# V of the second attention as one tile per head: 128x32 PV products, shared pools and a new table of rankings

## The chip, the cores and the metric

The kernel runs on one core of a Trainium2 chip. The core has five engines with instruction streams of their own: TensorE (PE; its weight loads are shown apart, as PEld), VectorE (DVE), ScalarE (ACT), GpSimd (POOL) and SyncE (SP), which here only issues transfers. Sixteen DMA engines move data between the device's memory (HBM) and the core's memory (SBUF, 128 partitions); PE writes its results to PSUM, eight banks of 128 partitions x 512 float32. The metric is the device time of one execution in microseconds (us); lower is better.

## What is computed (the reference)

Two attention blocks with caches, A and B, on 16 sequences of 32 tokens, model width 1024, 32 query heads of 128. A has 4 heads of keys and values, each used by 8 query heads; B has 32. The cache has 1024 keys per head. All inputs are bfloat16.

```python
def ref(x, k_cache, v_cache, wq, wo):        # A: 4 kv heads repeated 8 times, B: 32
    q = (x @ wq).reshape(B, Sq, H, Dh).transpose(0, 2, 1, 3)
    scores = einsum("bhqd,bhkd->bhqk", q, k) * (Dh ** -0.5)
    p = softmax(scores, axis=-1)
    o = einsum("bhqk,bhkd->bhqd", p, v)
    return o.transpose(0, 2, 1, 3).reshape(B, Sq, H * Dh) @ wo
out = concatenate([ref_A, ref_B], axis=-1)
```

B's keys and values are most of the bytes: 16 x 32 x 1024 x 128 x 2 bytes = 134 MB each. Nothing of them is used twice.

## The kernel before, in words

The work of both attentions is cut into quads: four (sequence, head) combinations of 32 tokens, whose scores fill 128 partitions x 1024 keys, two PSUM banks. Each attention has 128 quads. A quad's steps are: scores (PE; scoresA at L1003, scoresB at L1035), negative maximum (DVE, L1046), exponential with row sum (ACT, L1059), transposition of P (PE, L1071 for A and L1105 for B), evacuation of P^T to SBUF (ACT or DVE, L659), PV (PE, L1091 for A and L1124 for B), reciprocal (DVE, L1173), normalisation by the row sum (ACT L1182 or DVE L1183), transposition of O (PE, L1190 for A and L1198 for B), and evacuation into OTA_sb or OTB_sb (L659). When a group is complete, its output projection follows (oproj, L831), added up over blocks in `acc` (L843, L852, L847). Query projections (L743, L762), the transposition of A's keys on PE (L977) and a reshuffling of B's queries (L773, L786) are spread over the steps.

B's quads go in pairs (pairB). A pair holds two sequences x four heads. Its K comes as four tiles of 512 KB, each of two adjacent heads: 1024 keys of a head on 64 partitions, 16 keys per partition. Such a tile is transposed in place by DVE in blocks of 32x32 (L984). V comes in the same shape, four tiles of two heads each (st_dmaVB, tile_src). So PV works on tiles of 64 partitions: `st_pvB` runs, for each of 16 key chunks, four products with 64x64 weights from P^T and 256 columns of V (two heads of one tile side by side). Half of each result belongs to the wrong head; the transposition of O (two products with `rowsel`, a masked identity) picks the right half. Both quads of a pair share P2_sb and PT2_sb. The last pair has a version of its own, `st_last` (L1143, L1161, L1162, L1165): it takes V in halves so that part of the projection can start before the last tiles are there.

SBUF holds 8 slots of K and 6 of V for B. From pair 51 (LATE) on, space that is no longer needed (wq_sb, xT_sb, half of QT_sb) gives four more homes to K and four to V (home_k, home_v). All loads are issued by SP in one queue, in a fixed order: a load that has to wait for its slot keeps back all that follow it. `load` writes each transfer such that one descriptor reads 16 KB (V) or 8 KB (K) of contiguous HBM.

The order on every engine, and who takes a step that ACT or DVE could take, is decided when the program is built. `list_schedule` replays the program with a table of durations (DUR, PACKET, DMA_FIRST and so on), counts instruction fetches of PE in blocks (FETCH_BLOCK, FETCH_US), and takes at each step the ready operation with the highest rank; banks and slots of the pools (SLOTS) are handed out in that replay. There are 16 variants of the rank (RANKS); TUNE names the variant for each stretch of 77 operations (WINDOW).

```python
SLOTS = {"bank": 8, "P": 2, "P2": 1, "PT": 2, "PT2": 2, "stat": 8, "O": 2, "O2": 3}
turn = len(order) // WINDOW
turn = TUNE[turn] if turn < len(TUNE) else 0
```

Of the kernel before, what the change touches and what calls it, by code (L numbers as in the profile page):

```python
# [30 lines left out]
PE_MODE = {"scoresB": 2, "Qshuf": 2, "Qshuf2": 2, "PVB": 3, "PVBh": 3}  # L31
MODE_IN = 0.094
MODE_OUT = {0: 0.0, 2: 0.18, 3: 0.1}
PE_INSTR = {"scoresB": 32, "scoresA": 2, "PT_trA": 8, "PT_trB": 8, "PVA": 16, "PVB": 32, "PVBh": 32, "OT_tr": 2, "OT_trB": 4, "KTA_tr": 16, "Qshuf": 16, "Qshuf2": 16,
            "qprojA": 4, "qprojB": 4, "oprojA": 4, "oprojB": 4, "xT_tr": 16}
FETCH_BLOCK = 252
FETCH_US = 6.2
# [9 lines left out]
TUNE = (6, 7, 1, 5, 6, 8, 8, 8, 8, 8, 8, 11, 5, 15, 1, 9, 0, 1, 5, 1, 7, 14,  # L47
        15, 12, 12, 10, 12, 12, 15, 3, 12, 14, 7, 13, 13, 13, 13, 13, 7, 6, 10, 1, 12, 10,
        3, 12, 0, 11, 9, 12, 7, 13, 12, 11, 12, 3, 4, 10, 14, 9, 9, 10, 4, 0, 0)
# [11 lines left out]
    "scoresB": (0.232, 0.20), "scoresA": (0.216, 0.20), "PT_trA": (0.48, 0.22), "PT_trB": (0.48, 0.22), "PVA": (0.45, 0.22), "PVB": (0.437, 0.22), "PVBh": (0.22, 0.22),  # L61
    "OT_tr": (0.056, 0.22), "OT_trB": (0.112, 0.22), "KTA_tr": (0.45, 0.22), "Qshuf": (0.39, 0.20), "Qshuf2": (0.235, 0.20), "qprojA": (0.432, 0.20), "qprojB": (0.432, 0.20),
    "oprojA": (0.432, 0.20), "oprojB": (0.432, 0.20), "xT_tr": (0.45, 0.22),
    "exp": (1.10, 0.12), "PT_ev@act": (0.466, 0.13), "norm@act": (0.25, 0.13), "normB@act": (0.36, 0.13), "OT_ev@act": (0.11, 0.13), "OTB_ev@act": (0.17, 0.13), "KTA_ev@act": (0.466, 0.13),
    "qA_ev@act": (0.47, 0.13), "qB_ev@act": (0.478, 0.13), "QR_ev@act": (0.478, 0.13), "acc0@act": (0.47, 0.13), "acc0@dve": (0.58, 0.12), "xT_ev@act": (0.90, 0.13),
    "o_fin@act": (0.47, 0.13),
    "KBt_tr": (1.15, 0.11), "max": (1.12, 0.11), "recip": (0.06, 0.11), "norm@dve": (0.265, 0.13), "normB@dve": (0.40, 0.13), "PT_ev@dve": (0.58, 0.12),
    "OT_ev@dve": (0.13, 0.12), "OTB_ev@dve": (0.2, 0.12), "KTA_ev@dve": (0.58, 0.12), "QBt_tr": (0.345, 0.10), "acc+": (0.58, 0.12), "accF": (0.59, 0.12),
    "qA_ev@dve": (0.58, 0.12), "qB_ev@dve": (0.58, 0.12), "xT_ev@dve": (0.60, 0.12), "o_fin@dve": (0.58, 0.12), "QR_ev@dve": (0.58, 0.12),
# [3 lines left out]
PACKET = {"kb_dma": (4096, 0.1592), "vb_dma": (4096, 0.1592), "outh_dma": (1024, 0.049), "wqh_dma": (1024, 0.049)}  # L73
PACKET_DEFAULT = (2048, 0.0847)
DMA_ISSUE = 0.45
DMA_FIRST = 1.4
DMA_LAST = 0.8


def dma_time(op):  # L80
    size, us = PACKET.get(op.name, PACKET_DEFAULT)
    return op.dur / size * us / 16
# [32 lines left out]
SLOTS = {"bank": 8, "P": 2, "P2": 1, "PT": 2, "PT2": 2, "stat": 8, "O": 2, "O2": 3}  # L115
# [12 lines left out]
class Prog:  # L128
# [120 lines left out]
    def list_schedule(self, lat=0.05, look=LOOK):  # L249
# [137 lines left out]
        dma_free = [0.0]  # L387
# [7 lines left out]
        pe_pos = [0]  # L395
        pe_have = {0: 0.0, 1: 0.0}

        def fetch_wait(i, st, commit=False):
            if ops[i].eng != "pe" or not FETCH_US:
                return 0.0  # L400
            n_ = PE_INSTR[ops[i].name]
            p0 = pe_pos[0]
            ex = 0.0
            b = p0 // FETCH_BLOCK + 1
            while b * FETCH_BLOCK <= p0 + n_ - 1:
                tb = st + ex + ops[i].dur[0] * (b * FETCH_BLOCK - p0) / n_
                a = pe_have.get(b, 0.0)
                if a > tb:
                    ex += a - tb
                    tb = a  # L410
                if commit:
                    pe_have[b + 1] = tb + FETCH_US
                b += 1
            if commit:
                pe_pos[0] = p0 + n_
            return ex
# [136 lines left out]
def build(nc, pa, pb, out):  # L553
# [34 lines left out]
    with stack:  # L588
# [21 lines left out]
        VB_sb = sb("VB_sb", [P, NVB, 16 * Dh], BF)  # L610
# [4 lines left out]
        P2_sb = sb("P2_sb", [P, SLOTS["P2"], 2 * Sk], BF)  # L615
        PT2_sb = sb("PT2_sb", [P, SLOTS["PT2"], Sk], BF)
        O2_sb = sb("O2_sb", [P, SLOTS["O2"], 2, Dh], BF)
        rowsel = sb("rowsel", [P, 2, P], BF)
        PT_sb = sb("PT_sb", [P, SLOTS["PT"], NCH, P], BF)
# [25 lines left out]

        pr.add("pool", lambda g: g.memset(rowsel[:], 0.0), writes=["rowsel"], name="c0")
        for r_ in range(4):
            pr.add("pool", lambda g, r_=r_: g.tensor_copy(rowsel[32 * r_:32 * r_ + 32, r_ % 2, 32 * r_:32 * r_ + 32], ident[32 * r_:32 * r_ + 32, 32 * r_:32 * r_ + 32]),
                   reads=["ident"], writes=["rowsel"], name="c1")
# [102 lines left out]
        def qprojB(m_, G):  # L752
# [5 lines left out]
            for j0 in range(0, DJ, JS):  # L758
# [6 lines left out]
                pr.add("pe", e_qp, reads=ws + [("xT", 1, G)] + ([("xV", 0), ("xV", 1)] if m_ == NMSB - 1 else []), writes=[v], claims=[("Qtok", (m_ * NG + G) % NQT)], name="qprojB", dur=0.225 * JS,  # L765
# [148 lines left out]
        def st_dmaKB(x):  # L914
            if x < 2 * NIT:
                kind, sl = home_k(x)
                pr.step, was = 2 * ((x - NKB) // 4) if x >= NKB else pr.step, pr.step
                pr.add("sp", lambda e: load(e, tile_k(x), tile_src("k", x), 2), writes=[(kind, sl)], dma_key=f"{kind.lower()}{sl}", name="kb_dma",
# [8 lines left out]
        def home_v(x):  # L927
            if x >= V_LAST:
                return ("KB", kb_of(x - 8))
            if x < XV:  # L930
                return ("VB", x % NVB)
            r = (x - XV) % (NVB + 4)
            return ("xV" if r < 2 else "QV", r % 2) if r < 4 else ("VB", (XV + r - 4) % NVB)
# [10 lines left out]

        def tile_k(x):
# [3 lines left out]
        def tiles_v(x, w):  # L949
            kind, sl = home_v(x)  # L950
            if kind == "xV":
                return xT_sb[:, 1, :, :].rearrange("p (i j) t -> p i (j t)", i=2)[:, sl:sl + w, :]
            if kind == "QV":
                return QT_sb[:, 0, :, :, :].rearrange("p (i b) a q -> p i (b a q)", i=2)[:, sl:sl + w, :]
            return (KB_sb if kind == "KB" else VB_sb)[:, sl:sl + w, :]

        def tile_v(x):
            return tiles_v(x, 1)[:, 0, :]

        def st_dmaVB(x):  # L960
            kind, sl = home_v(x)
            pr.step, was = 2 * ((x - NVB) // 4) if x >= NVB else pr.step, pr.step
            pr.add("sp", lambda e: load(e, tile_v(x), tile_src("v", x), 4), writes=[(kind, sl)],
                   dma_key=f"{kind.lower()}{sl}", name="vb_dma", dur=2 * Sk * Dh * 2, wtag={(kind, sl): ("V", x)})
# [18 lines left out]
        def st_ktrB(x):  # L983
            pr.add("dve", lambda e: e.transpose(tile_k(x).bitcast(F32), tile_k(x).bitcast(F32)),  # L984
                   writes=[home_k(x)], name="KBt_tr", rtag={home_k(x): x}, wtag={home_k(x): ("T", x)})
# [8 lines left out]
        def st_scoresA(q):  # L994
# [3 lines left out]
            if True:  # L998
# [3 lines left out]
                for u in range(2):  # L1002
                    pr.add("pe", lambda e, u=u: e.matmul(bank(vS[u]), qt[:, q.b, q.hh0:q.hh0 + 4, :].rearrange("p a q -> p (a q)"),  # L1003
                                                         KTA_sb[:, sl, u * 512:(u + 1) * 512], start=True, stop=True),
                           reads=[("QT", q.s % 2, q.hh0 + a) for a in range(4)] + [("KTA", sl)] + ([("QV", 0), ("QV", 1)] if q.s == NSB - 2 else []), writes=vS, name="scoresA", dur=0.225,
                           tag="A%d" % q.t, rtag=dict([(("QT", q.s % 2, q.hh0 + a), q.s) for a in range(4)] + [(("KTA", sl), q.kid)]))

        def p2_of(v):
            return P2_sb[:, v.idx, :] if isinstance(v, Virt) else xT_sb[:, v[1], :, :].rearrange("p j t -> p (j t)")[:, 0:2 * Sk]

        def pt2_of(v):
            return PT2_sb[:, v.idx, :] if isinstance(v, Virt) else xT_sb[:, v[1], :, :].rearrange("p j t -> p (j t)")[:, (1 + v[2]) * Sk:(2 + v[2]) * Sk]

        def pt2_chunk(vPT, c, e0, n0):
            return pt2_of(vPT[c // 8]).rearrange("p (m r two) -> p m r two", m=4, two=2)[e0:e0 + 64, c // 2 % 4, n0:n0 + 64, c % 2]

        def st_scoresB(qs):
            n = qs[0].pn
            vP, vPT = (("xT", 0, 0), (("xT", 0, 1), ("xT", 0, 2))) if n >= XT_FREE and n % 2 else (Virt("P2"), (Virt("PT2"), Virt("PT2")))
            for q in qs:  # L1020
                score_buf(q)
                q.vP, q.vPT, q.vO = vP, vPT, Virt("O2")
# [17 lines left out]
            for fp_ in range(4):  # L1040
                pr.add("pe", lambda e, fp_=fp_: e_s(e, fp_), reads=qr + [r_ for r_, _ in kt], writes=[r_ for q in qs for r_ in q.vS],
# [7 lines left out]
        def st_exp(q):  # L1049
            vS, vP, vst = q.vS, q.vP, q.vst  # L1050

            def emit(e):
                if q.pi == 0:
                    src = both(vS).rearrange("p u (c k) -> p k u c", c=NCH // 2)
                    dst = P_sb[:, vP.idx, :].rearrange("p (k u c) -> p k u c", u=2, c=NCH // 2)
                else:
                    src = both(vS).rearrange("p g (s j) -> p g j s", s=16)
                    dst = p2_of(vP)[:, q.e * Sk:(q.e + 1) * Sk].rearrange("p (g j s) -> p g j s", g=2, s=16)
# [5 lines left out]
        def st_ptr(q):  # L1064
            vP, vPT, vb = q.vP, q.vPT, q.vbt

            def e_pt(e):
                last = None
                p32 = P_sb[:, vP.idx, :].bitcast(F32)
# [3 lines left out]
            pr.add("pe", e_pt, reads=[vP, "id32", vPT], writes=[vb], name="PT_trA")  # L1073

        def st_pev(q, eng=None):
            vPT, vb = q.vPT, q.vbt
            evac(lambda: PT_sb[:, vPT.idx, :, :].rearrange("p c q -> p (c q)").bitcast(F32), lambda: bank(vb), reads=[], writes=[vb, vPT],
                 name="PT_ev", eng=eng)

        def ptc_of(vPT, c, lo, hi):  # L1080
            return PT_sb[:, vPT.idx, :, :].rearrange("p c q -> p (c q)").rearrange("p (m r two) -> p m r two", m=NPK, two=2)[:, c // 2, lo:hi, c % 2]
# [329 lines left out]
```

## Time and profile before

| what | value |
|---|---|
| device time, three runs | 848.25, 849.33 and 853.75 us, median 849.33 |
| profiled execution | 848.89 us, with a span of 847.1 us from first to last instruction |
| granted TensorE clock | 1.00 |
| read from HBM | 337.64 MB, 401 GB/s over the span |
| idle before ACT L1059 (exponential) | 62.0 us, 58.2 of it waiting for DVE L1046 |
| DVE L1046, maxima | 256 of 1210 ns |
| DVE L984, transposition of K | 240 of 1220 ns in KB_sb, 16 of 1218 ns in wq_sb |

The page of the profile gives each engine's busy time and share of the span, the span in 40 slices, and the costliest groups of instructions by line. In a row of a group stand the line, the engine, the operation, output and inputs, how often, total busy us and mean ns of one, and then the idle time before the group and what ended it. The table of stretches gives for each stretch the busy us of PE, PEld, DVE, ACT and POOL (with counts), the granted clock, the mean busy share of the DMA engines, and GB/s. "SPq" is the queue of transfers that SP issues. A row of the table of waits reads: who waited, for whom, us in total, times, longest.

### The profile page before, as it was taken

What the parts mean: (1) busy time and instruction counts of PE and PEld (TensorE: products, weight loads), DVE (VectorE), ACT (ScalarE), POOL (GpSimd) and SP (SyncE); (2) the same over time, 40 slices, a digit from 0 to 9 for tenths busy, and PEclk for the clock granted to TensorE, in tenths of its full rate; (3) what the DMA queues carried; (4) which work ended last, traced back from release to release, by engine and by line L of the source; (5) the groups of instructions that cost most, each with busy time, mean ns of one, the idle gap of its engine ahead of it and who ended that gap; (6) DMA issues with size and microseconds to landing.
All of it is one profiled execution on the core that took longest, in us unless ns stands there. A gap on an engine that the chain in (4) does not pass through costs nothing.

```text
span 847.1 us, 29624 instructions
## 1 busy us (share of the span) xinstructions
PE 765.6 (90%) x12931; PEld 520.5 (61%) x13056; DVE 725.5 (86%) x1018; ACT 623.8 (74%) x1363; POOL 6.1 (1%) x20
## 2 busy tenths in 40 slices
PE   6989989899898999898999988989899998899878
PEld 4456655666565566565666665666666665666655
DVE  1499977979898898987999898997999979998995
ACT  3497786778777777786788787577877868686874
POOL 1000000000000000000000000000000000000000
PEclk9999999999999999999999999999999999999999
DMA  9999999999999999999999999999999999999995
GB/s 339 424 416 421 409 403 370 419 401 400 416 393 400 408 404 418 419 407 410 422 390 411 417 378 425 419 410 392 417 408 412 412 414 415 421 414 415 421 426 214
DMA packets 52816, 341.68 MB, mean 403 GB/s; under 512 B 12048, under 2 KB 12304, under 8 KB 21968
## 3 DMA queue, kind: packets, MB, share of 16 engines
q1 hardware_dynamic: 52128, 337.95, 98.0%
q8 instruction: 103, 1.69, 0.7%
q0 software_dynamic: 560, 1.84, 0.5%
q14 instruction: 25, 0.20, 0.1%
HBM read 337.64 MB, written 2.10 MB: 401 GB/s over the span
## 4 chain that ended last, share of the span: by engine, by line
PE 55%; DVE 26%; ACT 14%; issue 3%; DMA 1%; SPq 0%; DVEq 0%; ACTq 0%
DVE stat L1046 12%; PE psum L1124 10%; PE psum L831 9%; DVE KB_sb L984 9%; ACT P_sb L1059 8%; PE psum L1035 6%; PE psum L762 5%; PE psum L1071 5%; PE psum L743 5%; PE psum L1105 4%; PE psum L1091 4%; PE psum L1003 4%; ACT PT_sb L659 2%; ACT O_sb L1182 2%; DVE wq_sb L984 1%
## 5 line engine op out<-in xcount | busy, mean ns | idle before, releaser
L1046 DVE TENSOR_REDUCE stat<-psum 128x1 f32<-128x1024 f32 x256 | 303.8, 1210 | 53.8 <-PE psum L1003 30.4
L1059 ACT ACTIVATE P_sb<-psum,stat 128x1024 bf16<-128x1024 f32 x246 | 276.0, 1123 | 62.0 <-DVE stat L1046 58.2
L984 DVE STREAM_TRANSPOSE KB_sb<-KB_sb 128x1024 f32<-128x1024 f32 x240 | 285.6, 1220 | 4.0 <-DMA KB_sb<-in_B_k_cache_dram 4.0
L659 ACT COPY PT_sb<-psum 128x512 f32<-128x512 f32 x226 | 131.4, 603 | 34.3 <-PE psum L1071 21.8
L1124 PE MATMUL psum<-VB_sb,PT_sb 64*64 64x256 bf16 x3584 | 116.4, 271 | 9.1 <-ACT P_sb L1059 5.3
L1124 PEld LDWEIGHTS psum<-VB_sb,PT_sb 64*64 64x64 bf16 x3584 | 96.9, 107 | 28.4 <-issue 26.2
L1182 ACT ACTIVATE O_sb<-psum,stat 128x128 bf16<-128x128 f32 (+1 forms) x205 | 80.7, 416 | 41.2 <-PE psum L1091 21.2
L1071 PE MATMUL psum<-id,P_sb 128*128 128x128 f32 x512 | 88.0, 296 | 6.9 <-ACT P_sb L1059 4.2
L1071 PEld LDWEIGHTS psum<-id,P_sb 128*128 128x128 f32 x512 | 73.8, 208 | 24.0 <-ACT P_sb L1059 12.8
L1091 PE MATMUL psum<-VA_sb,PT_sb 128*128 128x128 bf16 x1024 | 77.9, 219 | 6.9 <-ACT PT_sb L659 1.8
L1035 PE MATMUL psum<-KB_sb,QR 32*32 32x512 bf16 x3840 | 73.2, 394 | 9.4 <-ACT P_sb L1059 4.6
L1091 PEld LDWEIGHTS psum<-VA_sb,PT_sb 128*128 128x128 bf16 x1024 | 62.3, 98 | 30.6 <-issue 10.8
L1105 PE MATMUL psum<-id,P_sb 128*128 128x128 f32 x472 | 75.8, 285 | 4.8 <-ACT P_sb L1059 3.5
L1003 PE MATMUL psum<-KTA_sb,QT_sb 128*128 128x512 bf16 x214 | 72.1, 380 | 5.1 <-ACT P_sb L1059 1.6
L1105 PEld LDWEIGHTS psum<-id,P_sb 128*128 128x128 f32 x472 | 63.5, 193 | 17.3 <-ACT P_sb L1059 7.5
L762 PE MATMUL psum<-wq_sb,xT_sb 128*128 128x512 bf16 x228 | 66.0, 392 | 6.0 <-issue 2.4
L831 PE MATMUL psum<-woB_sb,OTB_sb 128*128 128x512 bf16 x236 | 62.4, 379 | 4.5 <-ACT P_sb L1059 1.9
L1035 PEld LDWEIGHTS psum<-KB_sb,QR 32*32 32x32 bf16 x3840 | 43.9, 89 | 35.8 <-ACT P_sb L1059 7.6
L831 PE MATMUL psum<-woA_sb,OTA_sb 128*128 128x512 bf16 x240 | 59.9, 380 | 2.1 <-issue 0.8
L743 PE MATMUL psum<-xT_sb,wq_sb 128*128 128x512 bf16 x173 | 50.0, 379 | 3.9 <-issue 2.3
L1059 ACT ACTIVATION_READ_ACCUMULATOR P_sb<-psum,stat 128x1 f32 x246 | 50.4, 205 | 0.0
L843 DVE TENSOR_TENSOR acc<-acc,psum 128x512 f32<-128x512 f32 x64 | 41.3, 675 | 8.9 <-PE psum L831 8.7
(74 smaller groups left out, 719.8 us busy)
## 6 DMA issues: line engine op xcount, KB each, us to landing
KB_sb<-in_B_k_cache_dram SPq DMA_DIRECT2D x240, 512.0 KB, 8.4
VB_sb<-in_B_v_cache_dram SPq DMA_DIRECT2D x234, 512.0 KB, 7.5
KA_sb<-in_A_k_cache_dram SPq DMA_DIRECT2D x64, 256.0 KB, 7.7
VA_sb<-in_A_v_cache_dram SPq DMA_DIRECT2D x64, 256.0 KB, 7.6
wq_sb<-in_B_wq_dram SPq DMA_DIRECT2D x16, 512.0 KB, 8.0
woB_sb<-in_B_wo_dram SPq DMA_DIRECT2D x32, 256.0 KB, 8.1
woA_sb<-in_A_wo_dram SPq DMA_DIRECT2D x32, 256.0 KB, 6.1
wq_sb<-in_B_k_cache_dram SPq DMA_DIRECT2D x16, 512.0 KB, 11.7
```

Source lines behind the costliest of these rows:

```text
L659: return e.copy(dst, src) if hasattr(e, "activation") else e.tensor_copy(dst, src)
L762: last = e.matmul(bank(v)[:, 0:CW], xT_sb[:, 1, j, G * P:(G + 1) * P], wq_sb[:, j, mh * CW:(mh + 1) * CW], start=(j == 0), stop=(j == DJ - 1))
L831: last = e.matmul(bank(v)[:, 0:OUTW], OT[:, gp, hh, :], wo_[:, hh, oh * OUTW:(oh + 1) * OUTW], start=(hh == 0), stop=(hh == nh - 1))
L984: pr.add("dve", lambda e: e.transpose(tile_k(x).bitcast(F32), tile_k(x).bitcast(F32)), writes=[home_k(x)], name="KBt_tr", rtag={home_k(x): ...
L1003: pr.add("pe", lambda e, u=u: e.matmul(bank(vS[u]), qt[:, q.b, q.hh0:q.hh0 + 4, :].rearrange("p a q -> p (a q)"), KTA_sb[:, sl, u * 512:(u ...
L1035: last = e.matmul(bank(q.vS[g2])[32 * x:32 * x + 32, :].rearrange("p (s j) -> p s j", s=16), lhsT, rhs, start=(fp == 0), stop=(fp == 3), t ...
L1046: pr.add("dve", lambda e: e.tensor_reduce(stat[:, vst.idx, 0:1], both(vS), AXIS.XY, ALU.max, negate=True), writes=vS + [vst], name="max")
L1059: return e.activation(dst, src, ACTF.Exp, bias=stat[:, vst.idx, 0:1], scale=1.0, accum_out=stat[:, vst.idx, 1:2])
L1071: last = e.transpose(bank(vb)[:, m * P:(m + 1) * P], p32[:, m:Sk // 2:NPK], id32[:])
L1091: last = e.matmul(bank(vb)[:, 0:Dh], ptc_of(vPT, c, 0, P), VA_sb[:, kvs, c, :], start=(c == 0), stop=(c == NCH - 1))
L1105: last = e.transpose(bank(vb)[:, m * P:(m + 1) * P], p32[:, 4 * h + m:Sk:8], id32[:])
L1124: last = e.matmul(bank(q.vbo)[n0:n0 + 64, 0:2 * Dh].rearrange("p (i d) -> p i d", i=2), pt2_chunk(vPT, c, e0, n0), v2[e0:e0 + 64, :, c, :] ...
```

## The change

V of B is loaded one head at a time: 256 KB on 128 partitions, 8 keys per partition, as A's V is. A slot of V is split into two half slots, each with a semaphore of its own; NVB stays 6, so the bytes held are the same, and so it is with the late homes. The last pair's V goes into halves of K slots, which get a second resource name (KBh). PV is done per quad, with 8 chunks of keys x 4 products, each with 128x32 weights and 128 columns, in the four 32-column strips of the array. Each product then has the right head only, so O is transposed as in A, by one product with the identity, and rowsel is gone. B's quads use the same functions as A's for P^T and O, one at a time. P and P2 become one pool of 4 tiles, PT and PT2 one of 4, O and O2 one of 5; late in the kernel, every second pair still takes P and P^T from xT_sb. `st_last` is removed; the last pair goes as the others. V loads are asked for per quad, four at a time. The table of durations and the replay's figures for transfers and fetches are changed, and TUNE has other entries; RANKS and WINDOW stay.

```diff
-PE_INSTR = {"scoresB": 32, ..., "PVB": 32, "PVBh": 32, "OT_tr": 2, "OT_trB": 4, ...
+PE_INSTR = {"scoresB": 32, ..., "PVB": 64, "OT_tr": 2, ...
-TUNE = (6, 7, 1, 5, 6, 8, 8, 8, 8, 8, 8, 11, 5, 15, 1, 9, 0, 1, 5, 1, 7, 14,
+TUNE = (1, 7, 0, 14, 9, 2, 13, 15, 3, 10, 12, 11, 2, 6, 11, 8, 0, 6, 11, 2, 10, 7,
...
-SLOTS = {"bank": 8, "P": 2, "P2": 1, "PT": 2, "PT2": 2, "stat": 8, "O": 2, "O2": 3}
+SLOTS = {"bank": 8, "P": 4, "PT": 4, "stat": 8, "O": 5}
...
-        VB_sb = sb("VB_sb", [P, NVB, 16 * Dh], BF)
+        VB_sb = sb("VB_sb", [P, 2 * NVB, NCH * Dh], BF)
...
-            pr.add("sp", lambda e: load(e, tile_v(x), tile_src("v", x), 4), writes=[(kind, sl)],
-                   dma_key=f"{kind.lower()}{sl}", name="vb_dma", dur=2 * Sk * Dh * 2, wtag={(kind, sl): ("V", x)})
+            pr.add("sp", lambda e: load(e, tile_v(y), pb["v"][q.b0 + x // 2, q.m * MS + 2 * (x % 2) + q.e].rearrange("(p s) d -> p (s d)", s=NCH), 8),
+                   writes=[(kind, sl)],
+                   dma_key=f"{kind.lower()}{sl}", name="vb_dma", dur=Sk * Dh * 2, wtag={(kind, sl): ("V", y)})
...
-        def st_pvB(qs):
+        def st_pvB(q):
+            vPT, vb = q.vPT, q.vbo
...
+            def e_pv(e):
+                for c in range(NCH):
+                    for x in range(4):
+                        last = e.matmul(bank(vb)[32 * x:32 * x + 32, 0:Dh], ptc_of(vPT, c, 32 * x, 32 * x + 32), tile_v(4 * q.t + x)[:, c * Dh:(c + 1) * Dh],
+                                        start=(c == 0), stop=(c == NCH - 1), tile_position=(0, 32 * x))
                 return last
...
             for q in qs:
                 st_max(q)
                 st_exp(q)
-            st_ptB(qs)
-            if 4 * n == V_LAST:
-                st_last(qs)
-                return
-            st_pvB(qs)
-            while v_next[0] < min(V_LAST, 4 * n + 4 + NVB + (4 if n >= LATE else 0)):
-                st_dmaVB(v_next[0])
-                v_next[0] += 1
-            for q in qs:
+                st_ptr(q)
+                st_pev(q)
+                st_pvB(q)
+                while v_next[0] < min(2 * V_LAST, 4 * q.t + 4 + 2 * NVB + (8 if n >= LATE else 0)):
+                    st_dmaVB(v_next[0])
+                    v_next[0] += 1
                 st_recip(q)
                 st_norm(q)
                 st_otr(q)
```

In the built program the instructions of PE go from 13056 products to 12864; ACT takes 221 of the 256 evacuations of P^T (226 before) and 220 of the 256 norms (207 of 258 before), and SP issues 1002 transfers (746 before).

233 lines of the change are left out of this document (83 added, 150 removed).

## The prediction

> **What bounds the kernel now.** I read the page's slices first, then a table of stretches, then who the DMA-issuing queue waits for, then the end of the timeline.
>
> ```profile
> span 847.1 us, 29624 instructions
> PE 765.6 (90%) x12931; PEld 520.5 (61%) x13056; DVE 725.5 (86%) x1018; ACT 623.8 (74%) x1363; POOL 6.1 (1%) x20
> ...
> DMA packets 52816, 341.68 MB, mean 403 GB/s; under 512 B 12048, under 2 KB 12304, under 8 KB 21968
> ...
> q1 hardware_dynamic: 52128, 337.95, 98.0%
> ```
>
> The one load queue (q1) keeps the 16 DMA engines occupied for 98% of the span, more than PE (90%) or DVE (86%), and the bytes are the same before and after. So the end is set by how fast 342 MB come in, plus the head before the stream and the tail behind it. But an occupied DMA engine need not be a fast one:
>
> ```profile
> 0.00:20.00 20.00, 13.56 (x95) 8.18 (x97) 2.52 (x4) 8.11 (x9) 2.21 (x13) 1.00 0.93 333
> 20.00:820.00 800.00, 731.11 (x12372) 498.62 (x12491) 705.73 (x984) 601.92 (x1321) 2.85 (x5) 1.00 1.01 410
> 400.00:420.00 20.00, 18.68 (x282) 13.47 (x274) 17.80 (x25) 15.59 (x37) 0.00 (x0) 1.00 1.02 424
> 700.00:820.00 120.00, 103.04 (x2004) 74.56 (x1985) 113.84 (x154) 92.85 (x211) 2.17 (x4) 1.00 1.01 418
> 820.00:847.10 27.10, 20.95 (x470) 13.75 (x470) 17.21 (x31) 13.73 (x34) 1.08 (x2) 1.00 0.64 263
> 120.00:124.00 4.00, 3.67 (x47) 2.57 (x49) 4.00 (x8) 3.95 (x11) 0.00 (x0) 1.00 0.99 412
> 126.00:128.00 2.00, 1.95 (x18) 1.61 (x18) 1.94 (x5) 1.82 (x8) 0.00 (x0) 1.00 0.92 307
> 140.00:143.00 3.00, 2.95 (x24) 2.20 (x22) 3.00 (x4) 2.84 (x9) 0.00 (x0) 1.00 1.07 314
> ```
>
> The last two columns are the DMA share and GB/s; the first five pairs of numbers are the engines, and the granted clock (1.00) never moves. The share stays near 1 while the rate falls to 307 and 314. The issuing queue shows why:
>
> ```profile
> 116.93 1.24 SPq L628 DMA_DIRECT2D KB_sb<-in_B_k_cache_dram  x2
> 125.67 2.77 SPq L628 DMA_DIRECT2D VB_sb<-in_B_v_cache_dram  x4
> ```
>
> From 118.2 to 125.7 us SP issues nothing; the work queued ahead runs out near 126 us, and packets that start on an emptied engine take longer, so they count as busy. The dip is starvation in disguise. Who holds SP up:
>
> ```profile
> SPq L628 <- PE psum L1124: 104.4, 42, 7.5
> SPq L628 <- PE psum L977: 38.3, 15, 5.2
> SPq L628 <- PE psum L1190: 38.2, 21, 4.3
> SPq L628 <- PE psum L1035: 36.2, 18, 5.0
> ```
>
> Most of its waiting is for L1124, the PV product of the second attention (B), which frees four V tiles (2 MB) at once. So the kernel is bound by DMA, and what can be gained is the gap between 410 GB/s and the 424 of a stretch that never starves.
>
> **The profiled run.** Its time is 848.89 us, 1.8 more than its span, and 0.4 under the median of 849.33. The sum is made against 848.9.
>
> **The change, part by part.**
>
> PV on PE. The rows of today:
>
> ```profile
> 0.00:847.10 847.10, 126.41 (x4032) 105.22 (x4032) 1.00 0.99 403
> ...
> 412.83 1.69 PEld L1124 LDWEIGHTS psum<-VB_sb,PT_sb 64*64 64x64 bf16 x64
> 412.84 1.94 PE L1124 MATMUL psum<-VB_sb,PT_sb 64*64 64x256 bf16 x64
> 408.96 0.87 PEld L1035 LDWEIGHTS psum<-KB_sb,QR 32*32 32x32 bf16 x64 [0.42 <-issue]
> 408.96 1.19 PE L1035 MATMUL psum<-KB_sb,QR 32*32 32x512 bf16 x64
> 819.24 0.98 PEld L1091 LDWEIGHTS psum<-VA_sb,PT_sb 128*128 128x128 bf16 x16 [0.27 <-issue]
> 819.27 1.12 PE L1091 MATMUL psum<-VA_sb,PT_sb 128*128 128x128 bf16 x16
> ```
>
> (The first row is L1124 alone over the span.) A pair of quads takes 64 products of 256 columns in 1.94 us. Afterwards a quad takes 32 products of 128 columns, four side by side in 32-column strips. L1035 shows that four strips with different streams run side by side, and that a load of 32 weight columns takes 0.87/64 = 13.6 ns. So a quad takes 32 x 13.6 = 0.44 us of loads and, as with L1035, some 0.2 to 0.3 us until the last product ends: 0.65 us busy. 128 x 0.65 = 83 us replace 126.4 + 2.0 (the last pair, L1143): 45 us less. Both ends: at L1035's whole pace per instruction, 32/64 x 1.19 = 0.60 us (52 less); at L1091's pace, with nothing side by side, 32 x 1.12/16 = 2.24 us (158 more). I take 0.65, since L1035 has the strips. Today's groups enter with a gap (0.42 us in the row above); there will be 128 entries for 64, so 64 x 0.3 = 19 us come back, between nothing and 27. PE: about 26 us less.
>
> Transposes of O, norms, evacuations.
>
> ```profile
> L1198 PE MATMUL psum<-rowsel,O_sb 128*128 128x128 bf16 x252 | 28.0, 220 | 3.5 <-ACT O_sb L1182 1.9 <-DVE O_sb L1183 0.5
> L1190 PE MATMUL psum<-ident,O_sb 128*128 128x128 bf16 x128 | 27.9, 223 | 3.8 <-ACT O_sb L1182 2.0 <-DVE O_sb L1183 0.9 <-ACT OTB_sb L659 0.4
> L1182 ACT ACTIVATE O_sb<-psum,stat 128x256 bf16<-128x256 f32 x82 | 36.4, 474 | 17.1 <-PE psum L1124 14.3 <-DVE stat L1173 2.6
> L1182 ACT ACTIVATE O_sb<-psum,stat 128x128 bf16<-128x128 f32 x123 | 46.0, 378 | 24.1 <-PE psum L1091 21.2 <-DVE stat L1173 2.2 <-issue 0.2
> L659 ACT CAST OTB_sb<-psum 128x128 bf16<-128x128 f32 x108 | 25.7, 282 | 2.8 <-PE psum L1198 2.2
> L659 ACT COPY OTA_sb<-psum 128x64 f32<-128x64 f32 x111 | 24.5, 225 | 21.6 <-PE psum L1190 21.5
> ```
>
> 252 half transposes become 128 whole ones of 223 ns: 28.5 us for 28.0, nothing. Norms of 256 columns become norms of 128: 0.1 us each, and evacuations save 0.06 us each, on 126 quads: some 20 us, nearly all on ACT in the new order. DVE keeps its 256 maxima and 256 transposes of K and stays near 725 us. Neither engine sets the end, so these are worth nothing directly; they let P^T and O leave sooner.
>
> Loads of V. 256 loads of 512 KB become 512 of 256 KB, all of SP's queue. SP issues one in about 0.6 us (four in 2.4):
>
> ```profile
> 402.64 2.38 SPq L628 DMA_DIRECT2D VB_sb<-in_B_v_cache_dram  x4
> ```
>
> ```profile
> KB_sb<-in_B_k_cache_dram SPq DMA_DIRECT2D x240, 512.0 KB, 8.4
> ...
> KA_sb<-in_A_k_cache_dram SPq DMA_DIRECT2D x64, 256.0 KB, 7.7
> ```
>
> So 256 x 0.6 = 152 us of SP. It has that: its 746 transfers at 0.6 us are 448 us, and the other 400 are waiting. (The page's rows give count, size and microseconds from issue to landing.) A load of 256 KB occupies the DMA engines for 0.62 us at 424 GB/s, so SP just keeps up within a run of eight V loads and gets ahead on the K loads, 512 KB each. Every load also ends in small completion packets (12048 under 512 B, about 16 a load). Their price stands in no row; the trace's packet records have them at 9 ns, so 256 x 16 x 9 ns / 16 = 2.3 us more of a full queue. Ends: nothing, and twice that.
>
> Earlier release of V. The eight half tiles of a pair come free four at a time, after 0.65 us instead of 1.94, and the first four before the second quad's exponentials are transposed. The pools of P and P^T hold as many bytes as now but any quad may take any slot. Both shorten the 104 us that SP waits for L1124. How much rate that gives I can only bound: nothing (410) and all (424). I take 417, because in 700:820, where the kernel has four more homes for V and for K, so that space is less scarce, it runs at 418. 800 us x 410 GB/s = 328 MB; at 417 that takes 786.6 us: 13.4 less. Ends: 0 and 26.4 less.
>
> Head. The first V loads are issued ahead of K loads that come later in use; the head is set by x and Wq in the first 20 us at 333 GB/s, which stay first: 0, within 1 us either way.
>
> Tail. Today's special treatment of the last pair goes:
>
> ```profile
> 838.02 1.99 PE L1143 MATMUL psum<-KB_sb,xT_sb 64*64 64x128 bf16 x128
> ...
> 842.61 0.69 DVE L852 TENSOR_TENSOR acc<-acc,psum 128x512 bf16<-128x512 f32 x1 [0.26 <-PE psum L831]
> 843.21 1.28 DVE L847 TENSOR_TENSOR woA_sb<-acc,psum 128x512 bf16<-128x512 f32 x2
> ```
>
> From the last V to the last sum: 843.9 - 838.0 = 5.9 us (the 1.28 includes an overlap). Afterwards: 0.65 PV, 0.15 gap, 0.37 norm, 0.3 transpose, 0.3 evacuation, 1.7 for eight projection products, 0.9 for the last sum: 4.4 us. 1.4 less; ends 2.5 less and 1 more, since the projection's first half can no longer run ahead.
>
> **Sum.** 848.9 - 13.4 + 2.3 - 1.4 = 836.4. The PE, ACT and DVE terms are not added, as the stream hides them while it never starves; if the loads stopped being the bound, PE's 766 - 26 = 740 and DVE's 725 would come next.
>
> [...]
> [...] No row here has 128x32 tiles.
>
> **The rivals.**
>
> 1. Slower: PV strips run in turn. Place: the new PV line; price 2.24 us a quad (above). PE would then need 766 - 128 + 128 x 2.24 = 925 us, beyond the stream: with today's idle 81 us, near 1000. It decides from about 1.6 us a quad, where PE's 81 idle us are used up. For it: no row shows the tile form. Against: L1035's four strips. 5%.
> 2. Slower: SP becomes the pace. In runs of eight V loads, issue (0.6) against transfer (0.62) leaves no reserve, so each wait starves the engines at once. If that doubled half of today's loss of 26 us: 849 + 13 = 862. It decides once an issue takes more than 0.62 us. Against: SP now waits 400 of 847 us. 8%.
> 3. No gain: starving comes from K (L1035, L977) and from the order on PE, and SP, which issues strictly in order, is held by the next of these instead. Then 848.9 + 2.3 - 1.4 = 850. For it: three quarters of SP's waiting is not for L1124. 21%.
> 4. Full gain: starvation vanishes, 848.9 - 26.4 + 2.3 - 1.4 = 823. Against: stretches with Wq loads and instruction fetches do not reach 424. 14%.
>
> My forecast, part of the gap closed, has 52%.
>
> **How the numbers follow.** 836 is the forecast's. Its own range is 829 to 843. The range 827 to 851 reaches into the full gain (its upper half) and takes in no gain; rivals 1 and 2 and the rest of 4 are left out, under 20%. About 1% (8.5 us) is what a measurement of this kernel can tell from no change, so faster means below 841: 52 + 14 = 66%. Same, 841 to 858: 21%. Slower: 13%.
>
> **What would show it.** Right: the stretch 20:820 at 415 to 420 GB/s with fewer slices below 400; SP's waits for the new PV line well under 104 us; PV groups of 32 products in 0.6 to 0.7 us; PE about 740 us; an end within 10.5 us of the last V load's landing. Wrong: PV groups over 1.6 us (rival 1); SP issuing back to back while GB/s dips (2); as many slices below 400 with SP's waits moved to K and L977 (3).

## The result and the profile after

The changed kernel takes 1228.7 us (median of four runs, 1223.55 to 1252.26) where the kernel before takes 850.53: a ratio of 1.442, 95% interval 1.432 to 1.452. One of the four runs, 1252.26, counts as slow, over 2% above the fastest, and is not in the ratio. The forecast was 836, in a range of 827 to 851. The kernel is 378 us slower by the medians, and the forecast was wrong.

The page of the changed kernel, its head, the clock, the rate by slice and the DMA queue (slices of 30.6 us now):

```profile
span 1222.8 us, 29615 instructions
PE 832.5 (68%) x12731; PEld 532.5 (44%) x12864; DVE 739.1 (60%) x1029; ACT 611.9 (50%) x1348; POOL 5.0 (0%) x15
PEclk9998888787878898788888898888888778887767
GB/s 347 334 347 323 299 279 273 265 271 292 259 282 253 281 289 263 260 297 286 254 299 255 319 273 283 279 279 269 275 253 294 234 288 298 291 251 284 287 274 142
DMA packets 56913, 341.70 MB, mean 279 GB/s; under 512 B 16144, under 2 KB 16400, under 8 KB 26064
...
q1 hardware_dynamic: 56224, 337.97, 92.3%
```

The bytes are the same (341.7 MB) and the queue is still occupied for 92% of the span, but the rate is 279 GB/s against 403. No engine has become the bound: PE stands at 68%, DVE at 60%, ACT at 50%. The table of stretches (last three columns: granted clock, DMA share, GB/s) says that it is so from start to end:

```profile
0.00:20.00 20.00, 13.05 (x107) 8.11 (x109) 2.52 (x4) 9.03 (x11) 1.13 (x8) 1.00 0.92 327
20.00:820.00 800.00, 555.96 (x8453) 351.27 (x8542) 491.25 (x681) 411.15 (x909) 0.00 (x0) 0.85 0.94 285
700.00:820.00 120.00, 85.57 (x1390) 54.99 (x1397) 78.28 (x108) 63.60 (x144) 0.00 (x0) 0.87 0.92 274
820.00:1222.00 402.00, 263.52 (x4172) 173.10 (x4213) 245.29 (x344) 191.67 (x429) 3.92 (x7) 0.81 0.92 267
```

The first 20 us, in which few of V's loads run, are nearly as before (327 GB/s, before 333). Afterwards 410 has become 285. The granted clock falls to 0.81 to 0.87, but that is not the loss: in 820:1222 PE is busy for two thirds of the time only, and loads that run alone (below) are as slow, 264 GB/s, at a granted clock of 1.00. In the rows of DMA issues, the last number is the median time from issue to landing:

```profile
KB_sb<-in_B_k_cache_dram SPq DMA_DIRECT2D x240, 512.0 KB, 18.4
VB_sb<-in_B_v_cache_dram SPq DMA_DIRECT2D x468, 256.0 KB, 17.5
KA_sb<-in_A_k_cache_dram SPq DMA_DIRECT2D x64, 256.0 KB, 16.9
```

K's loads, which the change does not touch, now land after 18.4 us instead of 8.4, and KA's after 16.9 instead of 7.7. Whatever slows V slows all that is in flight beside it. The waits answer to that (who waited, for whom, us in total, times, longest), DVE's and PE's first rows, then SP's:

```profile
DVE KB_sb L986 <- DMA KB_sb<-in_B_k_cache_dram: 238.5, 105, 12.0
```

```profile
PE psum L1104 <- DMA VB_sb<-in_B_v_cache_dram: 114.7, 30, 9.7
```

```profile
SPq L628 <- PE psum L1104: 83.5, 44, 5.6
```

Before, the transposition of K (L984 there) waited for hardly anything from memory, and the waits list no wait of PV for a transfer:

```profile
DVE KB_sb L984 <- DMA KB_sb<-in_B_k_cache_dram: 4.0, 2, 3.5
```

Now DVE waits 238.5 us and PE 114.7 us for transfers. What the change was to do on PE it does, as the timeline (start, us) shows:

```profile
403.89 0.46 PEld L1104 LDWEIGHTS psum<-VB_sb,PT_sb 128*32 128x32 bf16 x32 [0.42 <-issue]
403.90 0.63 PE L1104 MATMUL psum<-VB_sb,PT_sb 128*32 128x128 bf16 x32
404.57 8.50 SPq L628 DMA_DIRECT2D VB_sb<-in_B_v_cache_dram  x8
```

This PV group of a quad takes 0.63 us, forecast 0.65; the four strips run side by side. Over the whole span a group takes 0.70 us, at a mean granted clock of 0.84.

The trace also holds a record of every DMA packet, with size and duration; the views group them only by size. Grouped by size they carry the loss. All times are of q1, divided by the 16 engines:

| packets | before, count and mean | sum | after, count and mean | sum | more |
|---|---|---|---|---|---|
| 16 KB (V of B) | 8192 of 634 ns | 324.8 us | 8192 of 982 ns | 503.0 us | 178.2 |
| 8 KB (K, A's K and V, both Wo) | 22528 of 318 ns | 447.5 us | 22528 of 394 ns | 554.8 us | 107.3 |
| 2 KB | 9216 of 87 ns | 50.3 us | 9216 of 100 ns | 57.4 us | 7.1 |
| 4 B (completions) | 11936 of 9 ns | 6.7 us | 16032 of 13 ns | 12.6 us | 5.9 |

That is 298.5 us more of occupied queue. The other 77 us of the span are idle engines: 7.7% of 1222.8 is 94 us, where it was 17 (2.0% of 847.1). V's packets have the size that they had, 16 KB, and take half as long again. What differs is where a packet goes: V was loaded with 4 KB per partition, so that one 16 KB descriptor filled four neighbouring partitions (the 4 in `load(..., 4)`); now it is 2 KB per partition, and one descriptor fills eight (the 8 in `load(..., 8)`).

### The profile page after: what moved, and what is told of

Read it like the earlier page. It is cut to its first block, busy times and chain, and to the rows that moved or that the text cites. A ratio compares the mean times of both kernels' runs of the same rounds, so it can differ in the third digit from the quotient of the medians.

```text
span 1222.8 us, 29615 instructions
## 1 busy us (share of the span) xinstructions
PE 832.5 (68%) x12731; PEld 532.5 (44%) x12864; DVE 739.1 (60%) x1029; ACT 611.9 (50%) x1348; POOL 5.0 (0%) x15
## 4 chain that ended last, share of the span: by engine, by line
DMA 56%; PE 22%; SPq 8%; DVE 6%; ACT 5%; issue 3%; DVEq 0%
DMA KB_sb<-in_B_k_cache_dram 24%; DMA VB_sb<-in_B_v_cache_dram 21%; SPq L628 7%; DMA wq_sb<-in_B_k_cache_dram 5%; PE psum L1071 5%; ACT P_sb L1059 3%; PE psum L826 3%; PE psum L1035 3%; DVE stat L1046 3%; DVE KB_sb L986 2%; PE psum L1104 2%; PE psum L1091 2%; PE psum L1005 2%; DMA VA_sb<-in_A_v_cache_dram 2%; DMA woB_sb<-in_B_wo_dram 2%
## 5 line engine op out<-in xcount | busy, mean ns | idle before, releaser
L986 DVE STREAM_TRANSPOSE KB_sb<-KB_sb 128x1024 f32<-128x1024 f32 x240 | 293.1, 1234 | 239.3 <-DMA KB_sb<-in_B_k_cache_dram 238.5
L1071 PE MATMUL psum<-id,P_sb 128*128 128x128 f32 x984 | 188.4, 329 | 53.2 <-ACT P_sb L1059 39.5
L1071 PEld LDWEIGHTS psum<-id,P_sb 128*128 128x128 f32 x984 | 153.2, 212 | 96.8 <-ACT P_sb L1059 62.2
L1120 ACT ACTIVATE O_sb<-psum,stat 128x128 bf16<-128x128 f32 x220 | 78.8, 371 | 179.9 <-PE psum L1091 81.1
L1104 PE MATMUL psum<-VB_sb,PT_sb 128*32 128x128 bf16 x3584 | 78.6, 240 | 114.1 <-DMA VB_sb<-in_B_v_cache_dram 110.2
L1091 PE MATMUL psum<-VA_sb,PT_sb 128*128 128x128 bf16 x1024 | 92.5, 244 | 48.9 <-DMA VA_sb<-in_A_v_cache_dram 30.6
L1104 PEld LDWEIGHTS psum<-VB_sb,PT_sb 128*32 128x32 bf16 x3584 | 60.1, 106 | 139.2 <-issue 127.2
L1035 PE MATMUL psum<-KB_sb,QR 32*32 32x512 bf16 x3840 | 84.8, 438 | 40.9 <-issue 13.9
L826 PE MATMUL psum<-woB_sb,OTB_sb 128*128 128x512 bf16 x236 | 68.7, 411 | 13.4 <-DMA woB_sb<-in_B_wo_dram 6.9
L1035 PEld LDWEIGHTS psum<-KB_sb,QR 32*32 32x32 bf16 x3840 | 44.9, 91 | 70.9 <-issue 28.2
L738 PE MATMUL psum<-xT_sb,wq_sb 128*128 128x512 bf16 x170 | 55.4, 422 | 3.4 <-issue 2.2
L1005 PEld LDWEIGHTS psum<-KTA_sb,QT_sb 128*128 128x128 bf16 x256 | 24.7, 112 | 68.0 <-ACT P_sb L1059 50.8
L1127 PE MATMUL psum<-ident,O_sb 128*128 128x128 bf16 x256 | 50.8, 245 | 5.0 <-ACT O_sb L1120 3.5
L654 ACT COPY OTA_sb<-psum 128x64 f32<-128x64 f32 x102 | 22.1, 220 | 62.2 <-PE psum L1127 61.7
L979 PE MATMUL psum<-ident,KA_sb 128*128 128x128 bf16 x512 | 45.4, 240 | 10.8 <-DVE acc L847 5.6
## 6 DMA issues: line engine op xcount, KB each, us to landing
KB_sb<-in_B_k_cache_dram SPq DMA_DIRECT2D x240, 512.0 KB, 18.4
KA_sb<-in_A_k_cache_dram SPq DMA_DIRECT2D x64, 256.0 KB, 16.9
VA_sb<-in_A_v_cache_dram SPq DMA_DIRECT2D x64, 256.0 KB, 17.6
```

The lines of the kernel that those rows point to most:

```text
L654: return e.copy(dst, src) if hasattr(e, "activation") else e.tensor_copy(dst, src)
L826: last = e.matmul(bank(v)[:, 0:OUTW], OT[:, gp, hh, :], wo_[:, hh, oh * OUTW:(oh + 1) * OUTW], start=(hh == 0), stop=(hh == nh - 1))
L1035: last = e.matmul(bank(q.vS[g2])[32 * x:32 * x + 32, :].rearrange("p (s j) -> p s j", s=16), lhsT, rhs, start=(fp == 0), stop=(fp == 3), t ...
L1071: last = e.transpose(bank(vb)[:, m * P:(m + 1) * P], p32[:, m:Sk // 2:NPK], id32[:])
L1091: last = e.matmul(bank(vb)[:, 0:Dh], ptc_of(vPT, c, 0, P), VA_sb[:, kvs, c, :], start=(c == 0), stop=(c == NCH - 1))
L1104: last = e.matmul(bank(vb)[32 * x:32 * x + 32, 0:Dh], ptc_of(vPT, c, 32 * x, 32 * x + 32), tile_v(4 * q.t + x)[:, c * Dh:(c + 1) * Dh], st ...
```

## The experiments

Eleven kernels were run. Two questions were asked: what makes the loads slow, and, once that is undone, where the forecast gain went. On the first there are two theories. P: descriptors over eight partitions make the loads slow. H: the rest of the change does. On the second there are two more. S: SP, which has 256 more loads to issue, sets the pace. O: the order of the work on the engines keeps the loads waiting.

**The change with descriptors over four partitions.**

```diff
-...rearrange("(p s) d -> p (s d)", s=NCH), 8),
+...rearrange("(p s) d -> p (s d)", s=NCH), 4),
```

> The changed kernel with one number different: a V load reads 8 KB per descriptor and lays it on 4 neighbouring partitions (fold 4, as A's K and V do) instead of 16 KB on 8 (fold 8). Nothing else differs, nor does the order of instructions. [...] Theory H (twice as many, half as large V loads; the per-head addresses in HBM; the new order and its waits): all of that is still there, so above 1150 us.

Measured: 851.51 us (before 851.82), ratio 0.999, interval 0.996 to 1.002. One digit takes back the whole loss, with layout, PV, pools, order and the 512 loads unchanged. Its page, its stretch 20:820, and V's issue row:

```profile
PE 750.6 (88%) x12864; PEld 473.6 (56%) x12864; DVE 725.7 (85%) x1029; ACT 606.4 (71%) x1348; POOL 5.1 (1%) x15
...
GB/s 338 421 413 405 416 419 416 415 406 406 418 419 357 411 416 414 408 365 414 370 419 418 411 416 418 407 406 404 383 403 391 417 418 417 419 403 416 418 419 230
DMA packets 65105, 341.70 MB, mean 402 GB/s; under 512 B 16144, under 2 KB 16400, under 8 KB 26064
```

```profile
20.00:820.00 800.00, 716.22 (x12309) 453.35 (x12311) 701.63 (x993) 585.36 (x1310) 2.85 (x5) 0.99 1.01 408
```

```profile
VB_sb<-in_B_v_cache_dram SPq DMA_DIRECT2D x468, 256.0 KB, 7.5
```

The rate is back at 408 and a load lands after 7.5 us. For P the author had expected 826 to 850 us at 410 to 424 GB/s: 851.51 is 1.5 us above that, and far from H's range. So the form of the descriptor is the cause of the 378 us; whether by its eight partitions or by its 16 KB, the next runs tell. And there is no gain either: 408 is not the 417 of the forecast.

**The kernel before, with V's descriptors over eight partitions.** V stays at 4 KB per partition, so a descriptor has 32 KB.

```diff
-load(e, tile_v(x), tile_src("v", x), 4)
+load(e, tile_v(x), tile_src("v", x), 8)
```

> The kernel before, with its 512 KB loads of V read in descriptors of 32 KB on 8 neighbouring partitions (fold 8) instead of 16 KB on 4. P: slow like the changed kernel, 1150 to 1300 us, about 280 GB/s. H: 849 us, since loads, addresses and order are those of before.

Measured, one run: 1304.38 us, 4 above P's range. Nothing of the change is in this kernel but the eight partitions, and it is slower still.

```profile
GB/s 340 377 313 285 284 278 253 276 233 269 248 261 252 249 258 248 243 251 270 247 259 265 257 246 251 257 249 266 247 255 233 251 279 261 265 263 272 287 280 114
```

Its 32 KB packets take 2076 ns on average (two of 16 KB took 1268 before), and the 8 KB packets, none of them changed, 393 (before 318).

**The kernel before, with A's K and V over eight partitions.** These are 128 loads of 256 KB, a tenth of the bytes.

```diff
-load(e, KA_sb[:, sl, :, :]..., 4)
+load(e, KA_sb[:, sl, :, :]..., 8)      # the same for VA_sb
```

> The kernel before, with A's K and V loads (128 of 256 KB, 33.5 MB) at fold 8 instead of 4. A dose: in the changed kernel 134 MB of V at fold 8 cost 378 us. P: a quarter of it, some 94 us, so 900 to 990 us. H: 849 us. A theory that only the large stream of B's V suffers: 849 to 860 us.

Measured, one run: 996.39 us, 145 more than the 851.82 of the kernel before, from a quarter as many bytes as V's (P had expected 900 to 990). These loads are spread over the span, one to five in each slice but the last, and the rate is lower nearly everywhere:

```profile
GB/s 327 359 351 353 354 346 349 339 349 356 334 353 352 364 335 333 359 333 370 352 342 298 362 407 327 353 333 325 371 329 337 352 343 335 349 330 299 380 404 199
```

The harm is more than in proportion (a quarter of 378 would be 94), and it reaches loads that were not changed: 8 KB packets take 377 ns instead of 318.

**Loads alone.** Only 48 loads from V per phase, with nothing else on the core; all of the attention is left out. The phases differ in the number of partitions and in how many of them one descriptor fills.

```diff
+PHASES = ((128, 4), (128, 8), (32, 8), (64, 8), (32, 4), (64, 4), (128, 1), (128, 8), (128, 4))
```

> No attention at all: only loads of V tiles, 48 of a kind queued behind each other, then a wait, then the next kind; the output is filled with zeros. Kinds in order (partitions, fold): 128/4, 128/8, 32/8, 64/8, 32/4, 64/4, 128/1, 128/8, 128/4. [...] P: 128/4 410 to 425 GB/s, 128/8 210 to 300; 32/8 about 107 GB/s (4 engines at 16 KB in 0.615 us), and 64/8 little more than 32/8, under 170. If instead a descriptor with 8 pieces is slow by itself: 32/8 about 65 and 64/8 twice that, 130. H: 128/8 as fast as 128/4.

Measured: 363.87 us. The table of stretches, each stretch inside one phase, in the order above (last columns: DMA share and GB/s):

```profile
10.00:35.00 25.00, 0.00 (x0) 1.00 1.01 387
46.00:80.00 34.00, 0.00 (x0) 1.00 1.01 264
96.00:116.00 20.00, 0.00 (x0) 1.00 0.25 100
128.00:162.00 34.00, 0.00 (x0) 1.00 0.50 147
170.00:198.00 28.00, 0.00 (x0) 1.00 0.32 94
206.00:222.00 16.00, 0.00 (x0) 1.00 0.70 205
236.00:258.00 22.00, 0.00 (x0) 1.00 1.04 376
272.00:316.00 44.00, 0.00 (x0) 1.00 1.01 272
326.00:350.00 24.00, 0.00 (x0) 1.00 1.02 386
```

On 128 partitions it is 387 GB/s with four partitions to a descriptor and 264 with eight, and so again at the end (386 and 272). The expectation had put the first at 410 to 425, so loads alone do not reach the 424 of the kernel's best stretch; the gap between the two forms is as expected. No engine was computing, so SBUF traffic of the computing engines has no part in it. Two rows speak on the reason. On 32 partitions the same 16 KB descriptor over eight partitions takes 640 ns (median of the packet records), about what 16 KB take over four (615 in the kernel before). So eight partitions are not slow as such. On 64 partitions it takes 887 ns, on 128 it takes 992. A load of 64 partitions has eight such descriptors, and a share of 0.50 is eight of sixteen engines that never pause, at 147 GB/s; with four partitions 64 gave 205, about the pace of SP's issuing (128 KB in 0.64 us). So the descriptor was slow in the loads over 64 and 128 partitions (887 and 992 ns) and not in those over 32. These rows do not tell the reach of the load from the number of engines at work with such descriptors (four, eight, sixteen), since both grow together. The two phases with four partitions on 32 and 64 partitions say less: their packets start on engines that have run empty (shares 0.32 and 0.70) and spread from 307 to 554 ns.

The trace does not name the DMA engine of a packet, and why the descriptor is slow on 64 and 128 partitions no run shows. P's figure for 64/8, little more than 32/8 and under 170 GB/s, was the author's estimate, from an assumption that no run shows; measured are 147 GB/s beside 100.

**Two more sizes.** The change with V's descriptors over two partitions (4 KB), and the kernel before with K's over four (16 KB, now 8 KB over two).

```diff
-...s=NCH), 8),
+...s=NCH), 2),
```

> The change with V's descriptors of 4 KB over two neighbouring partitions instead of 16 KB over eight; everything else as changed. [...] Rival F: folding as such costs, the more the more partitions a descriptor spans; then two would be quicker than four and 20:820 goes over 412 GB/s, under 845 us.

```diff
-load(e, tile_k(x), tile_src("k", x), 2)
+load(e, tile_k(x), tile_src("k", x), 4)
```

> The kernel before with K's descriptors of 16 KB over four partitions (now 8 KB over two); V as before. [...]

Measured: 849.48 us (before 852.26), ratio 0.998, interval 0.995 to 1.001; and 853.77, ratio 1.000, interval 0.996 to 1.004. For the first the author had expected 848 to 860 us if two partitions are as good as four, for the second 844 to 851 if 16 KB over four does K no harm. So two partitions are as good as four for V, and rival F, under 845 us, falls. K's 16 KB descriptors over four partitions do no harm either: were 16 KB slow as such, K would have slowed down as V did, and that was expected to exceed 900 us. There is a step between four partitions and eight, and none between two and four; its reason is not shown. The packet records agree: a 4 KB packet over two partitions takes 160 ns, one of 8 KB over four 312 (both medians).

**Where did the forecast gain go? Size of the packets.** The change with four partitions to a descriptor, for V and for K:

> The change with four-partition descriptors for V (8 KB) and for K (16 KB, now 8 KB over two partitions). If the rate of full packets were what is left to win, K's larger packets give 845 to 850 us against 851 of v_fold4. If the stream is held by starving (S or O), the time stays at 849 to 855, since bytes, order and issues are unchanged.

Measured: 849.8 us, ratio 1.001, interval 0.998 to 1.004. The time lies where the two expectations overlap, but the interval leaves room for 2 us of gain at most, so the rate of full packets is not where the 13 us went.

**S: SP's pace.** In v_fold4, SP's waits (the queue's own table) and a piece of its timeline, beside the stretches it lies in:

```profile
SPq L628 <- PE psum L1104: 55.4, 34, 4.2
SPq L628 <- PE psum L1127: 35.8, 28, 4.7
SPq L628 <- PE psum L979: 26.9, 14, 6.8
```

```profile
264.87 0.47 SPq L628 DMA_DIRECT2D KA_sb<-in_A_k_cache_dram  x1
265.38 0.60 SPq L628 DMA_DIRECT2D VA_sb<-in_A_v_cache_dram  x1
266.03 5.95 SPq L628 DMA_DIRECT2D VB_sb<-in_B_v_cache_dram  x8
272.02 2.51 SPq L628 DMA_DIRECT2D woB_sb<-in_B_wo_dram  x4
```

```profile
265.00:270.00 5.00, 4.35 (x146) 2.93 (x132) 2.83 (x5) 3.90 (x11) 0.00 (x0) 1.00 0.95 344
270.00:275.00 5.00, 4.89 (x63) 3.33 (x62) 5.00 (x6) 4.29 (x8) 0.00 (x0) 1.00 0.85 308
```

The wait for PV has fallen from 104.4 to 55.4 us, and all of SP's waits from 400 to 262. But here the rate dips to 308 while SP issues without a pause: fourteen loads of 256 KB in 9.7 us, which is 380 GB/s. That is the sign that the prediction had named for rival 2. To price this, the kernel before was given one transfer of 32 bytes ahead of each of its 256 V loads, so that SP issues about as often as after the change:

```diff
+            e.dma_start(tiny[x % P:x % P + 1, x // P, :], pb["x"][0, 0:1, 0:16]).then_inc(sems_tiny[0], 16)
             return load(e, tile_v(x), tile_src("v", x), 4)
```

> The kernel before, with one extra transfer of 32 bytes issued by SP ahead of each of the 256 loads of V, into a scratch tile that nobody reads: SP issues as often as in the changed kernel (1002), while bytes, order, slots and layout are those of before. S: SP's pace costs what the gain was, 6 to 20 us: 856 to 872. O: 849 to 853 us.

Measured: 855.15 us (before 850.64), ratio 1.005, interval 1.002 to 1.008, between the ranges of S and O; 408 GB/s in 20:820:

```profile
20.00:820.00 800.00, 730.64 (x12303) 497.00 (x12426) 702.82 (x981) 598.39 (x1314) 2.85 (x5) 1.00 1.00 408
```

So these extra issues cost some 4.5 us. They are cheaper than V loads, as the timeline shows, and the load behind one is cheaper too (without one ahead a load of V takes 0.59):

```profile
405.63 0.43 SPq L964 DMA_DIRECT2D tiny<-in_B_x_dram  x1
406.10 0.47 SPq L631 DMA_DIRECT2D VB_sb<-in_B_v_cache_dram  x1
```

Over the span SP's issue records add up to 463 us before, 529 here and 633 in v_fold4. So this run carries 66 of the 170 us that the change adds, and 4.5 us is likely a lower mark: in proportion it would be some 12 us, as an estimate, most of the 13.4 that the rate was to give. Then 192 of SP's loads (KA, VA, woA, woB) were moved from v_fold4's SP to another engine, once to ACT and once to POOL:

```diff
+            if name in ('ka_dma', 'va_dma', 'woA_dma', 'woB_dma'):
+                eng = "act"
```

> v_fold4, with the 192 loads of A's K and V and of both Wo issued by ACT's queue instead of SP's, at the same places of the built order; PE, DVE and the rest of ACT's order stay. Theory S (with V at 256 KB SP issues one load in 0.6 us against 0.62 us of transfer and so cannot make up for a wait; that ate the gain): SP is relieved of 115 us, the slices below 390 GB/s get fewer, 836 to 846 us. Theory O (the stream starves because the order on PE and DVE frees the slots late, whoever issues): 848 to 856 us. A third outcome, above 856, would mean that ACT now waits for slots itself and its own work is late.

```diff
+            if name in ('ka_dma', 'va_dma', 'woA_dma', 'woB_dma'):
+                eng = "pool"
```

> The same 192 loads from POOL, which has nothing else to do, so that no engine's work can be held up; but its loads are plain, 2 KB per descriptor, which the records have at 84 ns against 77 ns for a quarter of an 8 KB one: 50 MB of them cost 10 us more of a full queue. S: 842 to 852 us (8 less by SP, 10 more by the descriptors, give or take). O: 857 to 866 us.

Measured: 860.93 us with ACT, ratio 1.012, interval 1.007 to 1.016, and 857.54 with POOL, ratio 1.009, interval 1.006 to 1.011. Relief for SP brought nothing: its issue records fell by 108 us, to 525 and 526, but SP now waited 362 and 355 us instead of 262, and the rates in 20:820 were 404 and 408. The wait that grew is the one for PV (L1108 in these kernels), first with ACT, then with POOL:

```profile
SPq L631 <- PE psum L1108: 180.7, 51, 10.8
SPq L631 <- PE psum L1108: 177.2, 52, 8.1
```

So a freer SP stands and waits for V's slots. That is against S as the only cause, though neither run refutes it: POOL's variant pays for smaller packets as well, 10 us by the author's estimate (its loads have 2 KB descriptors; in the kernel before a 2 KB packet takes 84 ns, a quarter of an 8 KB one 78, both by the medians), and ACT's lies in the third outcome, above 856, whose reason is not seen in ACT's waits (its wait for the maxima is 43.8 us, in v_fold4 41.6).

**O: the order.** v_fold4 with the table of rankings of the kernel before, which was written for that kernel's operations.

```diff
-TUNE = (1, 7, 0, 14, 9, 2, 13, 15, 3, 10, 12, 11, ...
+TUNE = (6, 7, 1, 5, 6, 8, 8, 8, 8, 8, 8, 11, ...
```

> The change with four-partition descriptors for V, and the table of rankings of the kernel before (TUNE) put back; durations, pools and loads stay as changed. Two theories of why the change with descriptors of four partitions takes 851 us and not 836: S, the doubled number of V loads holds SP; O, the order of the work on the engines, which the rankings decide, keeps the loads waiting. SP issues the same 1002 transfers here. By S alone the ranking is no lever and the time stays within 3 us of v_fold4 (848 to 855). By O it moves by more than that, to either side: the old table was written for other operations, so a loss (858 to 880) is the likelier, and SP's waits for PE then grow from 262 us. If it is under 847, the new table itself was a loss.

Measured: 896.71 us (before 852.26), ratio 1.053, interval 1.046 to 1.061. With the same loads, packets and issues, 45 us hang on this table alone.

```profile
GB/s 330 422 408 401 396 419 418 378 311 403 418 379 386 413 418 369 308 341 408 282 418 419 393 319 419 411 415 349 359 341 419 417 416 419 418 407 340 403 334 105
```

```profile
SPq L628 <- PE psum L1104: 87.1, 43, 6.2
SPq L628 <- PE psum L1005: 37.6, 37, 4.5
```

Full slices still reach 418 to 422; the loss lies in slices of 282 to 349, and SP's wait for PV grows from 55.4 to 87.1. The loss is above the 858 to 880 that was expected. So the order can cost far more than the 13.4 us in question; that it costs v_fold4 anything with its own table is not shown by a table that is worse. Whether one exists with which v_fold4 reaches 836 was not tried. None of the eleven is faster than the kernel before by more than the measurement tells.

## Why the prediction was wrong, step by step

- **Bound by DMA.** Right, and the reason why one slow form of descriptor cost 378 us: there was no reserve in the stream to hide it. The queue was occupied for 98% of the span before. The dip at 126 us stands in the packet records too: the thirteen 16 KB packets of the kernel before that start in 126:128, behind SP's pause, take 1029 ns (median), those that start in 112:124 take 611.
- **Loads of V. This is the step that failed:** "A load of 256 KB occupies the DMA engines for 0.62 us at 424 GB/s". The 0.62 is bytes by rate, and took for granted that the rate depends on bytes. Alone, such a load's sixteen packets, for sixteen engines, took 992 ns each, not 620, and in the kernel it slowed K's as well. The row of KA_sb that stands ahead of this step, 256 KB in 7.7 us, is of a load of the same shape with four partitions to a descriptor, so it did not cover the step. The diff showed the 4 turned into 8, and the text gave it no price, not even a bound. Rivals 1 to 4 hold no transfer that gets slower; all chances went to cases in which V's bytes come as fast as before. The number of loads is not what cost the 378 us: v_fold4 has all 256 more of them and takes 851.51 us (before 851.82).
- **Small packets.** 2.3 us forecast; in v_fold4 9.0 against 6.7, so 2.3.
- **PV on PE.** Right. In v_fold4, L1104 is busy for 76.9 us in all, 0.60 a quad, against 126.4 of L1124 and 2.0 of the last pair (L1143): 51.5 less where 45 were forecast. PE as a whole stands at 750.6 us. The page of before lacks 125 products' records; before_k_fold4, which has the same work with all its records, shows 784.2. So it is 34 less; the forecast was 26. The rival of strips in turn, at 2.24 us a quad, is refuted: in the changed kernel 32 loads take 0.46 us inside 0.63 us of products.
- **ACT and DVE.** ACT 623.8 to 606.4 in v_fold4, 17 less (forecast 20); DVE 725.7 (forecast 725). Worth nothing, as forecast.
- **Earlier release of V, 417 GB/s.** This step failed as well, hidden behind the first: v_fold4 gives 408. The release is earlier, as SP's wait for PV shows (104.4 to 55.4 us), but its worth was not there. SP's waits fell by 138 us (400 to 262), and 256 more issues at 0.6 us take 154: in a span that stays the same, what SP no longer waits it issues. The prediction counted both numbers and did not set them against each other: SP's waiting was called a reserve and the end of it a gain, and the same 138 us can't be both. Without the slow descriptor the time would have been that of rival 3, 850 us, and between the first slice and the last there are five below 400, as many as before. But that is the number and not the mechanism, since SP's waits for the two lines that rival 3 named fell too (L1035 36.2 to 17.6 us; L977, now L979, 38.3 to 26.9). Rival 2's sign was there: an issue of V took SP 0.63 us on average, over the 0.62 at which that rival was to decide, and less than half of the added issuing cost 4.5 us in before_tiny. How the missing 13.4 us divide between SP's pace and the order stays open. The new table of rankings had no price in the sum.
- **Head and tail.** 332 GB/s in the first 20 us of v_fold4: nothing, as forecast. From the last pair's first PV to the end of the last sum it takes 5.6 us there (forecast 4.4):

```profile
842.19 0.63 PE L1104 MATMUL psum<-KB_sb,xT_sb 128*32 128x128 bf16 x32
...
843.29 0.63 PE L1104 MATMUL psum<-KB_sb,xT_sb 128*32 128x128 bf16 x32
...
846.50 1.28 DVE L842 TENSOR_TENSOR woA_sb<-acc,psum 128x512 bf16<-128x512 f32 x2 [0.65 <-PE psum L826]
```

The second quad's PV starts 1.1 us after the first; the forecast had counted one PV. Its figure for the kernel before is low too: the last sum's row starts at 843.21 and lasts 1.28, so the end is at 844.49 and not 843.9, and the 5.9 us are 6.5. By the same reading the tail got 0.9 us shorter, not 1.4. From the end of the last read to the end of the span it is 7.8 us by the packet records, 10.3 before, 2.5 less.

## What to carry to other kernels

When a load changes its layout, price its descriptors as new ones: how many neighbouring partitions one descriptor fills counted here beside size and bytes. In loads over 128 partitions four ran at 387 GB/s and eight at 264. A row of the trace covers a step only if it agrees in that too. And an engine that waits for half the time is not thereby free: before its waiting is given away twice, add what the change makes it do to what it no longer waits for.

## What the runs showed of the hardware

Descriptors over eight partitions harmed loads that are not folded so: with a tenth of the bytes in that form the kernel lost 145 us (one run), and the unchanged 8 KB packets rose from 318 to 377 ns. On 32 partitions the same descriptor ran at about full pace (640 ns for 16 KB, against 615 over four partitions). The busy share of the DMA engines shows none of it: 1.01 at 387 GB/s and 1.01 at 264. The granted clock was lower where PE was busy less: 0.84 over the changed kernel's span, where PE is busy for 68%, and 0.98 in v_fold4 at 88%; which causes which, no run shows. And loads issued from ACT's queue (860.93 us) were no better than the same loads from SP (851.51); why was not settled.
